# Gate logits of a two-level mixture of experts: products split over tokens and turned on VectorE, in place of products split over depth, a copy and a joining product

## The chip, the core and the metric

One core of one Trainium2 chip runs the whole kernel. The metric is device time in microseconds (us). Before the change the median of 3 runs is 469.96 us (469.8 to 470.32). The engines are TensorE (PE; its weight loads are shown apart as PEld), VectorE (DVE), ScalarE (ACT), GpSimd (POOL) and SyncE (SP). They run side by side, each through its own queue in order, and wait for one another by semaphores.

## What is computed

Multi-query attention over 8 batches of 384 tokens with 16 heads of 64, followed by a mixture of experts on the 3072 resulting tokens of width 1024, with 4 groups of 4 experts:

```python
scores = scale * q @ k.T                       # one k and v for all heads
attn = softmax(scores)
x = (attn @ v) as (3072, 1024)
g_logits = x @ w_group                         # 4 columns
g_idx, g_w = argmax and its softmax weight
e_logits = x @ w_expert[g_idx]                 # 4 columns for each of 4 groups
e_idx, e_w = argmax and its softmax weight
out[token] = g_w * e_w * relu(x @ w1[g_idx, e_idx]) @ w2[g_idx, e_idx]
```

For each token, therefore, 4 group logits and 4 x 4 expert logits are wanted: 20 numbers out of a depth of 1024. These 20 logits are what the change is about.

## The kernel before

**Tiling and stages.** A step `p` is one block of 128 tokens of one batch with all 16 heads (24 steps of 128 tokens): `b, st = divmod(p, 3)`. Within a step TensorE makes the scores in six pieces of 64 keys (`scores`, L251), ScalarE exponentiates each (L253), VectorE adds them up (L259, L261, L265), and TensorE multiplies the pieces of the step before by v (`values`, L290). `weigh` (L301) divides by the row sums and leaves x, transposed, in `xT`: partitions are 128 of the 1024 depth positions, then 8 such slices `ko`, then the 384 tokens of a batch. GpSimd makes a bf16 copy of it (L302).

**Expert work as filler.** From step 4 on each step ends with four or five *units* of the expert products of an earlier batch (`fill`): a first layer unit is 8 products of 128x384 and a relu on ScalarE (L416, L417), a second layer unit 8 products of 128x512 and a scaled copy on ScalarE (L424, L425). Each batch is run through one expert chosen by its first block of tokens; leftover tokens of other experts are gathered at the end.

**The gate before.** At the end of the second step of a batch (`st == 1`) three jobs are put between the last units, at the places n-3, n-2 and n-1 of n units (L611 to L617):

- `gate_a` multiplies xT by `gw`, the gate weights (8 slices of 128 x 32 columns, of which 20 are used and 12 are zero). The array is taken as four column groups of 32. The depth is what is split: group j takes slice j, then slice j + 4, over all tokens of the batch (L314). So the PSUM tile `gps` has, on partitions 32j to 32j+31, a part of the sum for every token. ScalarE copies it to `part` (L316).
- `gate_both` adds the four parts up and turns the result in one: for each block of 128 tokens a product with `part` as the weights and `sel` (four identities of 32 under one another) as the moving operand (L321). In `lps` the tokens are on the partitions. Then `choose_a` copies the first block's 20 logits to `L` (L368) and finds each token's expert (L330 to L334), and for the batch before, whose blocks 1 and 2 are now complete, `gate_logits` copies the other 40 and `gate_math` finds the expert and its weight (L373 to L391, with an exponential on ScalarE, L380).
- `counts` adds the choices up over the tokens by a product with ones (L342), ScalarE copies the counts (L346), and `choose_b` finds the commonest expert and starts to load its weights (L356 on).

The tile `xT` is one for all batches. A gate with `lo = 0, hi = 3` at batch b therefore reads block 0 of batch b and, in the same tile, blocks 1 and 2 of batch b-1, which is why one gate serves two batches. There are nine gates: for the first block alone (in step 2, as jobs between score and value products), seven full ones, and one for the last two blocks at the end (L625 to L628).

**PSUM.** `scores`, `gps`, `lps`, the counts and the units take their PSUM tiles in turn from one ring of three (`ps_s`): the fourth tile waits until the first has been read. The order is written out by hand (`manual_schedule`): each engine's queue holds its instructions in the order in which the program calls them.

**The head.** `load_first` loads k on ScalarE's queue (L123), and four pieces of the first q block on SyncE's (L127), followed by the other blocks (L129 on). TensorE runs warming products on ones meanwhile (L152, L451).

Of the kernel before, what the change touches and what calls it, by code (L numbers as in the profile page):

```python
# [9 lines left out]
FP32 = mybir.dt.float32  # L10
# [3 lines left out]
P = 128  # L14
ACTF = mybir.ActivationFunctionType
OP = mybir.AluOpType
AX = mybir.AxisListType.X
# [4 lines left out]
def kernel(  # L22
# [11 lines left out]
    nc = tc.nc  # L34
    B, H, S, D = q.shape
# [6 lines left out]
    ST = S // P  # L42
    KO = Dm // P
# [4 lines left out]
    CW = 512  # L48
# [27 lines left out]
    def side(shape, dtype, name):  # L76
        return ps_s.tile(shape, dtype, tag="s", name=name)
# [41 lines left out]
    def load_first():  # L119
        kt = pool.tile([P, ST, 2, D], FP32, tag="k", bufs=2, name="kn")  # L120
        qt = pool.tile([P, ST, HP, 2, D], FP32, tag="qraw", bufs=2, name="qn")
        for a in range(2):
            nc.scalar.dma_start(out=kt[:, :, a], in_=kn)  # L123
        for c in range(2):
            hs = slice(c * HC, (c + 1) * HC)
            for a in range(2):
                nc.sync.dma_start(out=qt[:, 0, hs, a], in_=qn[0, :, a, hs])  # L127
        for a in range(2):
            nc.sync.dma_start(out=qt[:, 1, :, a], in_=qn[1, :, a])  # L129
        k_raw[0], q_raw[0] = kt, qt  # L130
        load_k(1)
        load_v(0)
        for a in range(2):
            nc.sync.dma_start(out=qt[:, 2, :, a], in_=qn[2, :, a])
        qe_in = q[1].rearrange("(a hp) (st p) d -> st p a hp d", a=2, p=P)
        qe = pool.tile([P, HP, 2, D], FP32, tag="y", bufs=4, name="qe")
        for a in range(2):
            nc.sync.dma_start(out=qe[:, :, a], in_=qe_in[0, :, a])
        q_nat.append(qe)
# [150 lines left out]
                nc.tensor.matmul(out=o_ps[p][64 * a:64 * a + 64, c, :], lhsT=v_sb[b][r, j, :], rhs=pt[p, j][r, a, :], start=(j == 0), stop=(j == KB - 1))  # L290

    xT_all = pool.tile([P, KO, S], FP32, tag="xT", bufs=1, name="xT")
    part_all = pool.tile([P, S], FP32, tag="part", bufs=1, name="part")

    def weigh(p):
        b, st = divmod(p, ST)
# [6 lines left out]
        if st == ST - 1:  # L303
            nc.sync.dma_start(out=xb_dram[b], in_=xbf[b][:].rearrange("p k s -> p (k s)"))

    part, ohe_t, choice, logits, seen = {}, {}, {}, {}, {}

    def gate_a(b, lo, hi):
        n = (hi - lo) * P
        ps = side([P, CW], FP32, "gps")  # L310
        for r in range(2):
            for j in range(4):
                ko = 4 * r + j
                nc.tensor.matmul(out=ps[32 * j:32 * j + 32, 0:n], lhsT=gw[:, ko, :], rhs=xT[b][:, ko, lo * P:hi * P], start=(r == 0), stop=(r == 1), tile_position=(0, 32 * j))  # L314
        part[b] = part_all
        nc.scalar.copy(out=part[b][:, lo * P:hi * P], in_=ps[:, 0:n])  # L316

    def gate_b(b, lo=0, hi=ST):
        ps = side([P, ST, 32], FP32, "lps")
        for st in range(lo, hi):  # L320
            nc.tensor.matmul(out=ps[:, st, :], lhsT=part[b][:, st * P:(st + 1) * P], rhs=sel[:], start=True, stop=True)  # L321
        return ps

    first = {}

    def choose_a(b, ps):
        gate_logits(b, ps, 0, 1)
        L = logits[b][:, 0]
        mx = pool.tile([P, 5], FP32, tag="mx1", bufs=1, name="mx1")
        nc.vector.reduce_max(out=mx[:], in_=L, axis=AX)  # L330
        oh = pool.tile([P, 5, 4], FP32, tag="oh1", bufs=1, name="oh1")
        nc.vector.tensor_tensor(out=oh[:], in0=L, in1=mx[:].unsqueeze(2).to_broadcast([P, 5, 4]), op=OP.is_ge)
        ohe = pool.tile([P, 4, 4], BF16, tag="ohe1", bufs=1, name="ohe1")
        nc.vector.tensor_mul(out=ohe[:], in0=oh[:, 1:5, :], in1=oh[:, 0, :].unsqueeze(2).to_broadcast([P, 4, 4]))  # L334
        first[b] = ohe
# [26 lines left out]
        wts[b] = (w1, w2)  # L362
        choice[b] = idx

    def gate_logits(b, ps, lo, hi):
        if lo == 0:
            logits[b] = pool.tile([P, ST, 5, 4], FP32, tag="L", bufs=2, name="L")
        nc.vector.tensor_copy(out=logits[b][:, lo:hi].rearrange("p s a e -> p s (a e)"), in_=ps[:, lo:hi, 0:20])  # L368

    def gate_math(b):  # L370
        L = logits[b]
        mx = pool.tile([P, ST, 5], FP32, tag="mx", bufs=1, name="mx")
        nc.vector.reduce_max(out=mx[:], in_=L[:], axis=AX)  # L373
        mxb = mx[:].unsqueeze(3).to_broadcast([P, ST, 5, 4])
        oh = pool.tile([P, ST, 5, 4], FP32, tag="oh", bufs=1, name="oh")
        nc.vector.tensor_tensor(out=oh[:], in0=L[:], in1=mxb, op=OP.is_ge)
        dl = pool.tile([P, ST, 5, 4], FP32, tag="dl", bufs=1, name="dl")
        nc.vector.tensor_sub(out=dl[:], in0=L[:], in1=mxb)
        ex = pool.tile([P, ST, 5, 4], FP32, tag="ex", bufs=1, name="ex")
        nc.scalar.activation(out=ex[:], in_=dl[:], func=ACTF.Exp)  # L380
        ohe = pool.tile([P, ST, 4, 4], BF16, tag="ohe", bufs=1, name="ohe")
        nc.vector.tensor_mul(out=ohe[:], in0=oh[:, :, 1:5, :], in1=oh[:, :, 0, :].unsqueeze(3).to_broadcast([P, ST, 4, 4]))
        ohe_t[b] = ohe
        smx = pool.tile([P, ST, 5], FP32, tag="smx", bufs=1, name="smx")
        nc.vector.reduce_sum(out=smx[:], in_=ex[:], axis=AX)
        ri = pool.tile([P, ST, 5], FP32, tag="ri", bufs=1, name="ri")
        nc.vector.reciprocal(out=ri[:], in_=smx[:])
        tt = pool.tile([P, ST, 4], FP32, tag="tt", bufs=1, name="tt")
        nc.vector.tensor_mul(out=tt[:], in0=ri[:, :, 1:5], in1=ri[:, :, 0:1].to_broadcast([P, ST, 4]))
        gv = gate_all[:, b * GE:(b + 1) * GE, :].rearrange("p (g e) s -> p s g e", g=G)  # L390
        nc.vector.tensor_mul(out=gv, in0=ohe[:], in1=tt[:].unsqueeze(3).to_broadcast([P, ST, 4, 4]))  # L391
# [68 lines left out]
    def fill(n):  # L460
        while n > 0:
            if not units:
                if begun[0] >= B or begun[0] not in wts:
                    return
                units.extend(first_units(begun[0]))
                begun[0] += 1
            units.pop(0)()
            n -= 1
            ran[0] += 1
            if ran[0] == (FO + 2 * ST) * (B - 2) + FO:  # L470
                leftover_w1()
            if ran[0] == (FO + 2 * ST) * (B - 1):
                leftover_w2()

    def gate_both(b):
        ps = gate_b(b)
        choose_a(b, ps)
        gate_logits(b - 1, ps, 1, ST)
        gate_math(b - 1)

    def jobs_gates(b):
        if b == 0:
            return [lambda: gate_a(0, 0, 1), lambda: choose_a(0, gate_b(0, 0, 1)), lambda: counts(0, None)]
        return [lambda: gate_a(b, 0, ST), lambda: gate_both(b)]

    bound = {}
    oki = singles.tile([1, 1], I32, name="oki")
# [60 lines left out]
        leftover["w2"] = w2  # L548
    for p in range(NP):
        b, st = divmod(p, ST)  # L550
        jobs = jobs_gates(0) if p == 2 else []
        if p == 0 or p == ST or (st == 1 and 1 < b < B - 1):
            load_q(b + 1)
        for j in range(3):
# [47 lines left out]
        if p > ST:  # L602
            n = 5 if p in FIVES else 4
            steps = {}
            if p == NP - 1:
                bound_a()
            if st == 2:
                steps = {0 if b == 1 else 1: lambda: counts(None, b - 1)}
                if p == NP - 1:
                    steps = {0: lambda: (counts(None, b - 1), early_pair()), n - 1: bound_b}  # L610
            if st == 1:  # L611
                gate_a_, gate_b_ = jobs_gates(b)
                steps = {n - 3: gate_a_, n - 2: gate_b_, n - 1: lambda: counts(b, None)}
            for i in range(n):
                fill(1)
                if i in steps:
                    steps[i]()  # L617
# [4 lines left out]
    weigh(NP - 1)  # L622
    last = B - 1
    fill(2)
    gate_a(last, 1, ST)  # L625
    fill(1)
    gate_logits(last, gate_b(last, 1, ST), 1, ST)
    gate_math(last)  # L628
    fill(2)
    counts(None, last)  # L630
# [143 lines left out]
    with rare_block:  # L774
# [7 lines left out]
      with tc.If(ok < 1):  # L782
# [41 lines left out]
          nc.vector.memset(zero[:], 0.0)  # L824
          for b in range(B):
              xT_all = pool.tile([P, KO, S], FP32, tag="xT", bufs=1, name="xT")
              part_all = pool.tile([P, S], FP32, tag="part", bufs=1, name="part")
              xT[b] = xT_all
              for a in range(2):
                  nc.sync.dma_start(out=xT[b][a * D:(a + 1) * D], in_=xr[b, a])  # L830
              xg = pool.tile([P, KO, S], BF16, tag="xbf", bufs=2, name="xg")
              nc.vector.tensor_copy(out=xg[:], in_=xT[b][:])
              nc.sync.dma_start(out=xb_dram[b], in_=xg[:].rearrange("p k s -> p (k s)"))
              gate_a(b, 0, ST)
              gate_logits(b, gate_b(b), 0, ST)
              gate_math(b)
              for st in range(ST):
                  nc.sync.dma_start(out=outv[b, :, st, :], in_=zero[:])
# [33 lines left out]
```

## Time and profile before

| what | value |
|---|---|
| median time | 469.96 us |
| span of the profiled execution | 468.4 us |
| VectorE busy | 304.6 us, 483 instructions |
| ScalarE busy | 246.9 us, 360 instructions |
| gate products L314 | 144 records, 12.2 us, mean 456 ns |
| joining products L321 | 48 records, 6.2 us, mean 263 ns |
| ScalarE copies L316 | 9, 4.0 us, mean 445 ns |
| VectorE copies L368 | 16, 3.0 us, mean 186 ns |
| transposes on VectorE, 128x1024 (L243) and 128x384 (L233) | mean 1226 ns and 540 ns |
| granted TensorE clock | 0.996 |

How to read it: an fp32 product is two records of TensorE, since it runs in two passes; products on different column groups overlap, so that the sum of their records is more than the time that they take. The end of a product's record is modelled[...]; the distance from start to start is what a stream of products costs. In a row of cost groups the numbers after the bar are the busy time in us and the mean of one in ns, then the engine's idle time just ahead of these instructions and what ended most of it. In a timeline line, the start and the time are in us, "x16" counts the merged instructions, and the bracket gives the idle time of the engine before it and what released it.

### The profile page before, as it was taken

The page shows a single profiled execution, that of the slowest core. Times are in us where ns is not written, and L with a number is a line of the kernel's source. Part 1 is how long each engine was busy: PE and PEld are TensorE (multiplying, and loading weights), DVE is VectorE, ACT ScalarE, POOL GpSimd, SP SyncE. Part 2 cuts the span into 40 slices and gives each one's busy share as a digit, 9 for nine tenths or more (in the row PEclk, how much of TensorE's full clock was granted, in tenths as well). Part 3 has the DMA queues.
Part 4 walks back from the last instruction along what each step waited for, and adds up shares of the span by engine and source line. Part 5 has one row for each costly group of instructions (what it writes and reads, how often), then busy time and mean ns, then how long its engine had stood idle before and what let it go on. Part 6 is the DMA issues. An engine that isn't in the chain of part 4 may idle for free. (4 is left out here: it accounts for less than half of the span.)

```text
span 468.4 us, 9356 instructions
## 1 busy us (share of the span) xinstructions
PE 457.0 (98%) x3791; PEld 195.5 (42%) x3807; DVE 304.6 (65%) x483; ACT 246.9 (53%) x360; POOL 60.4 (13%) x83
## 2 busy tenths in 40 slices
PE   8999999999999999999999999999999999999992
PEld 6333434433443344433434334434344334444641
DVE  4999958585695586783695855964858836682500
ACT  2966646546455555555474564664555654623331
POOL 1004003000130003000030000300021000330000
PEclk9999999999999999999999999999999999999997
DMA  8787997969499492967879493994929831499992
GB/s 161 94 135 117 218 211 118 212 165 215 77 161 232 168 167 33 201 132 237 134 102 211 123 210 88 147 211 171 156 60 197 151 158 46 63 208 261 283 247 79
DMA packets 152163, 74.52 MB, mean 159 GB/s; under 512 B 120216, under 2 KB 138652, under 8 KB 152112
## 3 DMA queue, kind: packets, MB, share of 16 engines
q0 software_dynamic: 28416, 37.84, 47.1%
q1 hardware_dynamic: 122896, 35.81, 32.4%
q8 instruction: 32, 0.52, 0.5%
q10 hardware_dynamic: 800, 0.20, 0.2%
q14 instruction: 19, 0.16, 0.1%
HBM read 92.62 MB, written 19.01 MB: 238 GB/s over the span
## 5 line engine op out<-in xcount | busy, mean ns | idle before, releaser
L253 ACT ACTIVATE pt<-s 128x1024 f32<-128x1024 f32 x144 | 142.8, 1025 | 62.7 <-PE s L251 60.1
L251 PE MATMUL s<-qT,kT 64*64 64x512 f32 x1152 | 144.6, 597 | 0.3 <-ACT qT L229 0.2
L290 PE MATMUL o<-pt,v 64*64 64x512 f32 x1152 | 141.0, 590 | 0.0
L261 DVE TENSOR_TENSOR presum<-presum,pt 128x1024 f32<-128x1024 f32 x96 | 116.6, 1215 | 14.0 <-ACT pt L253 8.2
L416 PE MATMUL hps<-xbf,w 128*128 128x384 bf16 x512 | 89.5, 326 | 0.6 <-ACT hT L417 0.6
L424 PE MATMUL yps<-w,hT 128*128 128x512 bf16 x368 | 84.9, 379 | 0.8
L290 PEld LDWEIGHTS o<-pt,v 64*64 64x64 f32 x1152 | 43.4, 133 | 76.6 <-issue 76.1
L259 DVE TENSOR_TENSOR presum<-pt 128x1024 f32<-128x1024 f32 x24 | 29.1, 1212 | 66.8 <-ACT pt L253 66.6
L425 ACT ACTIVATE y<-yps,gsel 128x512 f32<-128x512 f32 x48 | 33.0, 687 | 67.8 <-PE yps L424 64.2
L416 PEld LDWEIGHTS <-w 128*128 128x128 bf16 x512 | 48.0, 99 | 44.1 <-issue 14.8
L251 PEld LDWEIGHTS s<-qT,kT 64*64 64x64 f32 x1152 | 38.9, 133 | 65.5 <-issue 52.6
L302 POOL CAST xbf<-xT 128x1024 bf16<-128x1024 f32 x24 | 25.0, 1041 | 294.7 <-DVE xT L301 294.7
L417 ACT ACTIVATE hT<-hps 128x384 bf16<-128x384 f32 x64 | 31.2, 488 | 56.1 <-PE hps L416 48.3
L424 PEld LDWEIGHTS <-hT 128*128 128x128 bf16 x384 | 36.5, 98 | 50.3 <-issue 8.5
L145 POOL DMA_DIRECT2D w<-in_moe_w_dram x36 | 24.8, 708 | 70.9 <-issue 52.4
L301 DVE TENSOR_TENSOR xT<-o,rinv 128x1024 f32<-128x1024 f32 x24 | 29.2, 1216 | 2.6 <-PE o L290 2.6
L280 DVE STREAM_TRANSPOSE rinv<-rc 128x1024 f32<-128x1024 f32 x24 | 29.9, 1245 | 0.8
L265 DVE TRANSPOSE_TENSOR_REDUCE fold<-presum 128x32 f32<-128x1024 f32 x24 | 29.6, 1232 | 0.0
L368 DVE COPY L<-lps 128x20 f32<-128x20 f32 (+1 forms) x16 | 3.0, 186 | 34.5 <-PE lps L321 34.5
L243 DVE STREAM_TRANSPOSE qT<-qraw 128x1024 f32<-128x1024 f32 x20 | 24.5, 1226 | 0.6
L209 ACT ACTIVATE qraw<-qraw 128x1024 f32<-128x1024 f32 x21 | 22.0, 1049 | 0.0
L273 PEld LDWEIGHTS sm<-fold,sel 64*64 64x64 f32 x192 | 7.2, 133 | 12.9 <-issue 12.9
(146 smaller groups left out, 166.5 us busy)
## 6 DMA issues: line engine op xcount, KB each, us to landing
w<-in_moe_w_dram POOLq DMA_DIRECT2D x36, 512.0 KB, 10.0
w<-in_moe_w_dram POOLq DMA_DIRECT2D x9, 2048.0 KB, 22.1
out_dram<-y SPq DMA_DIRECT2D x24, 512.0 KB, 4.0
qraw<-in_q_dram SPq DMA_DIRECT2D x56, 192.0 KB, 3.8
x_bf<-xbf SPq DMA_DIRECT2D x8, 768.0 KB, 4.3
v<-in_v_dram SPq DMA_DIRECT2D x16, 96.0 KB, 2.9
k<-in_k_dram SPq DMA_DIRECT2D x28, 48.0 KB, 2.7
qn<-in_q_dram SPq DMA_DIRECT2D x4, 256.0 KB, 4.8
```

Of the source, the lines that this page charges most:

```text
L251: nc.tensor.matmul(out=ps[64 * c:64 * c + 64, a, :], lhsT=kT[b][r, j * D:(j + 1) * D], rhs=qT[p][r, c * CW:(c + 1) * CW], start=True, stop ...
L253: nc.scalar.activation(out=t[:], in_=ps[:], func=ACTF.Exp, scale=scale)
L259: nc.vector.tensor_add(out=presum[p][:], in0=pt[p, 0][:], in1=pt[p, 1][:])
L261: nc.vector.tensor_add(out=presum[p][:], in0=presum[p][:], in1=pt[p, j][:])
L265: nc.vector.tensor_reduce(out=fold[p][:], in_=presum[p][:].rearrange("p a (n i) -> p (a n) i", i=32), axis=AX, op=OP.add, apply_transpose= ...
L280: nc.vector.transpose(out=t[:].rearrange("p (b i) -> p b i", i=32), in_=rc[:].rearrange("p c b -> p (c b)").unsqueeze(2).to_broadcast([P, ...
L290: nc.tensor.matmul(out=o_ps[p][64 * a:64 * a + 64, c, :], lhsT=v_sb[b][r, j, :], rhs=pt[p, j][r, a, :], start=(j == 0), stop=(j == KB - 1))
L301: nc.vector.tensor_mul(out=xT[b][:, :, ts], in0=o_ps[p][:].rearrange("p c (h n) -> p (c h) n", n=P), in1=rinv[p][:].rearrange("p (h n) -> ...
L416: nc.tensor.matmul(out=ps[:, 0:S], lhsT=w1[:, ko, fc * P:(fc + 1) * P], rhs=xb[:, ko, :], start=(ko == 0), stop=(ko == KO - 1))
L417: nc.scalar.activation(out=state["h"][:, fc, :], in_=ps[:, 0:S], func=ACTF.Relu)
L424: nc.tensor.matmul(out=ps[:], lhsT=state["h"][:, fo, st * P:(st + 1) * P], rhs=w2[:, fo, nh * CW:(nh + 1) * CW], start=(fo == 0), stop=(fo ...
L425: nc.scalar.activation(out=y, in_=ps[:], func=ACTF.Copy, scale=gs_of()[:, st:st + 1])
```

## The change

The gate product no longer splits the depth over the column groups but the tokens: group j takes, of each block of 128 tokens, the 32 tokens 32j to 32j+31 (the `rhs` view with `j=4, i=32`), and goes through all 8 depth slices, so that each group ends with whole sums. `gps` is then, in each 32x32 block, logits by tokens, and a VectorE transpose that works on 32x32 blocks turns it straight out of PSUM into `L`, with the tokens on the partitions. The copy to `part`, the joining product and the PSUM tile `lps` go. `L` has 32 columns a block instead of 20, and its readers take a view of 20. The gate becomes one job in place of two, at the place n-2. In the fallback path at the end, which isn't entered with these inputs, the same functions are called. Apart from this, one of the four first loads of q is issued from ScalarE's queue instead of SyncE's.

It is meant to take the joining product off TensorE and the copy off ScalarE.

```diff
         for c in range(2):
             hs = slice(c * HC, (c + 1) * HC)
             for a in range(2):
-                nc.sync.dma_start(out=qt[:, 0, hs, a], in_=qn[0, :, a, hs])
+                (nc.scalar if c and a else nc.sync).dma_start(out=qt[:, 0, hs, a], in_=qn[0, :, a, hs])
...
     def gate_a(b, lo, hi):
-        n = (hi - lo) * P
-        ps = side([P, CW], FP32, "gps")
-        for r in range(2):
+        ps = side([P, ST * 32], FP32, "gps")
+        for ko in range(KO):
+            rhs = xT[b][:, ko, :].rearrange("p (s j i) -> p j s i", j=4, i=32)
             for j in range(4):
-                ko = 4 * r + j
-                nc.tensor.matmul(out=ps[32 * j:32 * j + 32, 0:n], lhsT=gw[:, ko, :], rhs=xT[b][:, ko, lo * P:hi * P], start=(r == 0), stop=(r == 1), tile_position=(0, 32 * j))
-        part[b] = part_all
-        nc.scalar.copy(out=part[b][:, lo * P:hi * P], in_=ps[:, 0:n])
-
-    def gate_b(b, lo=0, hi=ST):
-        ps = side([P, ST, 32], FP32, "lps")
-        for st in range(lo, hi):
-            nc.tensor.matmul(out=ps[:, st, :], lhsT=part[b][:, st * P:(st + 1) * P], rhs=sel[:], start=True, stop=True)
+                nc.tensor.matmul(out=ps[32 * j:32 * j + 32, lo * 32:hi * 32], lhsT=gw[:, ko, :], rhs=rhs[:, j, lo:hi, :], start=(ko == 0), stop=(ko == KO - 1), tile_position=(0, 32 * j))
         return ps
+
+    def gate_logits(b, ps, lo, hi):
+        if lo == 0:
+            logits[b] = pool.tile([P, ST, 32], FP32, tag="L", bufs=2, name="L")
+        nc.vector.transpose(out=logits[b][:, lo:hi, :].rearrange("p s e -> p (s e)"), in_=ps[:, lo * 32:hi * 32])
...
-    def gate_logits(b, ps, lo, hi):
-        if lo == 0:
-            logits[b] = pool.tile([P, ST, 5, 4], FP32, tag="L", bufs=2, name="L")
-        nc.vector.tensor_copy(out=logits[b][:, lo:hi].rearrange("p s a e -> p s (a e)"), in_=ps[:, lo:hi, 0:20])
-
     def gate_math(b):
-        L = logits[b]
+        L = logits[b][:, :, 0:20].rearrange("p s (a e) -> p s a e", a=5)
...
-    def gate_both(b):
-        ps = gate_b(b)
+    def gates(b):
+        if b == 0:
+            choose_a(0, gate_a(0, 0, 1))
+            return
+        ps = gate_a(b, 0, ST)
         choose_a(b, ps)
         gate_logits(b - 1, ps, 1, ST)
         gate_math(b - 1)
-
-    def jobs_gates(b):
-        if b == 0:
-            return [lambda: gate_a(0, 0, 1), lambda: choose_a(0, gate_b(0, 0, 1)), lambda: counts(0, None)]
-        return [lambda: gate_a(b, 0, ST), lambda: gate_both(b)]
...
-        jobs = jobs_gates(0) if p == 2 else []
+        jobs = [lambda: gates(0), lambda: None, lambda: counts(0, None)] if p == 2 else []
...
             if st == 1:
-                gate_a_, gate_b_ = jobs_gates(b)
-                steps = {n - 3: gate_a_, n - 2: gate_b_, n - 1: lambda: counts(b, None)}
+                steps = {n - 2: lambda: gates(b), n - 1: lambda: counts(b, None)}
...
     fill(2)
-    gate_a(last, 1, ST)
-    fill(1)
-    gate_logits(last, gate_b(last, 1, ST), 1, ST)
+    gate_logits(last, gate_a(last, 1, ST), 1, ST)
     gate_math(last)
```

## The prediction

> **What bounds the kernel now.** I read the busy shares first, then the waits of TensorE, then the timeline around one gate, because a change of 2 us in a stage of 55 us shows in no average. From the page, with two of its rows of cost groups:
>
> ```profile
> span 468.4 us, 9356 instructions
> ...
> PE 457.0 (98%) x3791; PEld 195.5 (42%) x3807; DVE 304.6 (65%) x483; ACT 246.9 (53%) x360; POOL 60.4 (13%) x83
> ...
> L368 DVE COPY L<-lps 128x20 f32<-128x20 f32 (+1 forms) x16 | 3.0, 186 | 34.5 <-PE lps L321 34.5
> ```
>
> TensorE is busy 98% of the span and no other engine above 65%. VectorE sat idle 34.5 us ahead of the gate's copies (some 4.3 us for each of eight gates): it waits for the gate, not the gate for it. The view of waits agrees; TensorE's products wait 3.5 us in all, nearly all of it at the head and the tail, and its weight loads show one wait that recurs at the gates:
>
> ```profile
> PE hps L416 <- ACT hT L417: 0.6, 1, 0.6
> ...
> PEld s L251 <- ACT cnt L346: 4.3, 5, 0.9
> ```
>
> So time is TensorE's queue, and a change is worth what it takes out of that queue plus what it does to this wait. The timeline of the second batch's gate (start, duration, engine, line, operation, tiles) shows both:
>
> ```profile
> 67.83 1.50 PE L314 MATMUL gps<-xT,gw 128*32 128x384 f32 x16
> ...
> 69.26 1.47 PE L416 MATMUL hps<-xbf,w 128*128 128x384 bf16 x8
> 69.39 0.48 ACT L316 COPY part<-gps 128x384 f32<-128x384 f32 x1 [0.97 <-PE gps L314]
> 70.41 0.80 PEld L321 LDWEIGHTS lps<-sel,part 128*128 128x128 f32 x6
> 70.57 0.75 PE L321 MATMUL lps<-sel,part 128*128 128x32 f32 x6
> ...
> 71.36 0.18 DVE L368 COPY L<-lps 128x20 f32<-128x20 f32 x1 [3.23 <-PE lps L321]
> ...
> 72.70 0.22 DVE L378 TENSOR_TENSOR dl<-L,mx 128x60 f32<-128x60 f32 x1
> ...
> 72.95 0.25 ACT L380 ACTIVATE ex<-dl 128x60 f32<-128x60 f32 x1 [1.69 <-DVE dl L378]
> 73.11 0.47 ACT L417 ACTIVATE hT<-hps 128x384 bf16<-128x384 f32 x1
> 73.48 0.16 ACT L346 COPY cnt<-cps 128x16 f32<-128x16 f32 x1
> 73.63 0.21 PEld L251 LDWEIGHTS s<-qT,kT 64*64 64x64 f32 x8 [0.87 <-ACT cnt L346]
> ```
>
> A gate takes TensorE twice (L314 and L321), with an expert unit between to hide the copy. And from the joining product (L321) a chain runs through VectorE to `ex`, behind which ScalarE's relu (L417) stands, behind which the PSUM buffer of the second score tile (L251, 73.63) comes free.
>
> Single records of this gate, the starts only: gate products start in four waves of four at 67.828, 68.175, 68.497 and 68.820; so 0.322 us a wave of 384 columns. The last expert product before started at 67.572 and the first after at 69.258; less one expert pitch (0.163) the gate product costs **1.523 us**: four waves (1.288) and 0.235 for entering and leaving the 128x32 tile mode. For the joining product the same two starts are 70.406 and 71.156: **0.587 us**. The other six full gates repeat these to 0.005 us.
>
> **What the Trainium skill says.** TensorE: Matmul & The Clock Gate, Part 3 (Packing small matmuls): products on different column groups run together, some 4 ns apart. Here they start 7 ns apart, four to a wave, so it holds. TensorEngine Tiling (Array Packing), Key Properties: a change of tiling mode drains TensorE. The trace agrees: a 0.09 us hole on each side of the gate product. The first page again, Back-to-back issue gap: a warm product costs its columns over 2.4 GHz plus 2.5 ns. In fp32 the trace fits twice the columns: 128 give 0.1095 us a wave (first gate), 256 give 0.216 (last), 384 give 0.322. VectorE: DVE Perf Modes, The three transpose paths: VectorE turns 32x32 blocks only, which is all that is asked here; no run so far shows one that reads PSUM.
>
> **The change, part by part.**
>
> *Joining product (3 products, 6 records), ScalarE copy.* Seven full gates give back 0.587 each. In the first gate the joining product stands between score and value products (31.336 to 32.193, less 0.429 for a score pitch): 0.428. In the last, between w2 products (428.327 to 428.906, less 0.213): 0.366. The copies (9 x 0.445 = 4.0 us of ScalarE) I cost at nothing: an expert unit of 1.3 us hid each.
>
> *Gate product, same multiplications in narrower pieces.* Before: 2 depth halves x 2 fp32 passes = 4 waves of 384 columns. After: 8 depth slices x 2 passes = 16 waves of 96 columns. By the fit a wave takes 2 x 96 / 2.4 + 2.6 = 82.6 ns, so 1.322 in place of 1.288, and with the same 0.235 of mode changes 1.557. Two things could make a wave longer. Its four weight loads: a load's record lasts 110 ns, which as a limit is the upper bound. I don't take it, since the denominators' product (L273, 64 columns of weights) starts successive waves 28 ns apart though its load records last 133 ns; most of a record is latency. And the moving operand now comes in three pieces of 32 columns, 128 apart, which no product of before does; I take no cost and keep a doubled wave (165 ns) as the bound. First gate: 16 waves at about 28 ns (the L273 pitch) for four at 109.5, 0.45 against 0.44; last: 16 at 56 for four at 216, 0.90 against 0.86. Both cost nothing within 0.05 us.
>
> *VectorE.* The copies of 20 and 40 columns (173 to 199 ns) become transposes of 32 and 64. A transpose of 1024 columns takes 1.226 us and of 384 0.540, so 1.07 ns a column and 0.13 fixed: 0.165 and 0.20; with what copies from PSUM take for the fixed part (0.15 to 0.157) 0.19 and 0.22. Upper bound: the 384-column transpose, 0.54 each. I take the middle pair, +0.04 us in the chain. The reads of `L` now skip 12 of 32 columns; same element counts, nothing. In the first gate the choice moves ahead of two additions on VectorE, which runs without a gap there (29.2 to 34.9) and only changes order.
>
> *The wait that stays.* The gate moves to where the joining product was (one unit before the counts), so the chain starts from it. Before, from the last joining product (71.044) to the second score tile (73.636) is 2.592. After: the last gate wave's record should last about 0.25 (against 0.276), so VectorE starts some 0.03 sooner and ends 0.04 later; 2.60. Behind the gate TensorE resumes after 0.178 (0.08 stream, 0.094 drain, as at 69.258 for 384 columns) instead of 0.112, and all that it does until the score tile is the same; so the interval from gate to second score tile stays, and 0.06 more of mode change hides in the wait. Queued behind a longer chain: `ex`, the relu, the count's copy on ScalarE, and TensorE's scores behind these.
>
> *Sum.* Full gate: 0.587 + 1.523 - 1.557 + 0.06 = 0.61; seven are 4.28. First 0.43, last 0.366 - 0.01 = 0.36. Together 5.07 us of a queue that is the bound: 469.96 - 5.07 = **464.9 us**.
>
> *The moved load at the head* (a fourth piece of q issued by ScalarE instead of SyncE). Issued about 0.5 us sooner, but TensorE's own warm-up runs to 5.98 and its q products follow at a steady 0.109, so nobody waits. ScalarE's table load comes 0.5 later, still 2.5 us before its first copy at 6.95. Nothing. *The tail* keeps its number of expert units; one moves behind the leftover's steps.
>
> **Rivals.**
>
> *Waves bound by their loads* (110 ns): 16 x 0.0274 = 0.44 us a full gate, 3.1 in seven: 468.0. For it: wave and load alternate in the trace at 109.5 with 128 columns. Against: that is also the stream's time, and the L273 waves.
>
> *Slower than before: the split stream.* If three short pieces halve the reading rate, a full gate gains 1.32 us, 9.3 in all: 474.2. Nothing in the trace shows such a read, for or against. Akin: dispatch. The same TensorE page (Wait — 56ns, not 53.3ns?) gives 62 ns a product for its sequencer with hardware decode off; 64 records, less 16 issued ahead (the trace's lead is never over 17), would be 48 x 0.062 = 2.98 against 1.32: 476.6. Against: in the last product (L719) the sequencer reached the branch behind all 32 products 0.147 us after the first started; with 16 or 17 queued, the rest went out at some 10 ns each.
>
> *The chain takes it all.* With transposes of 0.54 from PSUM the chain grows by 0.71, TensorE waits that much longer for its score tile at seven gates, and the gain drops by 5.0: 469.9, no change. Against: copies from PSUM here cost what copies from SBUF cost (173 ns for 20, 170 for 32).
>
> *More than the sum.* One PSUM buffer and one ScalarE entry fewer a gate could shorten other waits; if the remaining wait (some 0.17 a gate) went as well, 463.7.
>
> **How the numbers follow.** Forecast 0.70; load-bound 0.12; more 0.06; slower 0.08; no change 0.04. The range takes in the load-bound case and the larger gain, 463.6 to 468.4, and leaves out 0.12. Faster by over 0.2% (below 469.0): 0.88; within: 0.04; slower: 0.08.
>
> **What would show it.** Right: 16 waves about 83 ns apart, 1.3 to 1.35 us from first to last gate start; no L321; transposes of about 0.2 us; second score tile about 2.6 us after the last gate wave; stages shorter by 0.6 us each. Wrong: waves at 110 or 165 ns; transposes over 0.35 us; a wait of TensorE ahead of the counts, for `ohe`; or head and tail of another length.

## The result and the profile after

The changed kernel takes **466.36 us** (median of 4 runs, 466.23 to 466.55), beside 469.98 for the kernel before (4 runs): a ratio of 0.9923, 95% interval 0.9905 to 0.994. It is faster by 3.6 us where 5.1 were forecast. Run again later, on another occasion and beside other runs of before, it took 466.09 against 470.46: 0.9912 (0.9897 to 0.9927), so 4.4 us.

The page of the changed kernel, the same rows as before (L318 is the transpose that took the place of the copy L368):

```profile
span 464.9 us, 10115 instructions
...
PE 452.9 (97%) x4175; PEld 197.6 (43%) x4191; DVE 305.4 (66%) x483; ACT 243.0 (52%) x351; POOL 60.4 (13%) x83
...
L318 DVE STREAM_TRANSPOSE L<-gps 128x32 f32<-128x32 f32 (+1 forms) x16 | 3.6, 227 | 27.9 <-PE gps L312 27.9
```

TensorE has 384 more matmul records and is still busy 4.1 us less; the joining product's line is gone. VectorE's 16 turns cost 0.6 us more than the 16 copies did. The timeline of the gate that was shown for before:

```profile
69.02 1.53 PE L312 MATMUL gps<-xT,gw 128*32 128x96 f32 x64
...
70.48 1.47 PE L407 MATMUL hps<-xbf,w 128*128 128x384 bf16 x8
...
70.62 0.22 DVE L318 STREAM_TRANSPOSE L<-gps 128x32 f32<-128x32 f32 x1 [2.59 <-PE gps L312]
...
71.39 0.24 DVE L318 STREAM_TRANSPOSE L<-gps 128x64 f32<-128x64 f32 x1
...
72.05 0.22 DVE L369 TENSOR_TENSOR dl<-L,mx 128x60 f32<-128x60 f32 x1
...
72.30 0.25 ACT L371 ACTIVATE ex<-dl 128x60 f32<-128x60 f32 x1 [2.68 <-DVE dl L369]
72.46 0.47 ACT L408 ACTIVATE hT<-hps 128x384 bf16<-128x384 f32 x1
...
72.83 0.16 ACT L342 COPY cnt<-cps 128x16 f32<-128x16 f32 x1
...
72.98 0.14 PEld L251 LDWEIGHTS s<-qT,kT 64*64 64x64 f32 x3 [0.88 <-ACT cnt L342]
```

One visit of TensorE instead of two, and the chain dl, ex, relu, score tile as before, now starting from the gate product. The view of TensorE's waits has one new entry, at the end of the kernel:

```profile
PE pb L674 <- DMA xe<-x_bf: 0.5, 1, 0.5
```

Where the gain was made and lost is best seen in the two traces laid over one another, counted from the first score product of each, at the first score product of a step:

```
gain against before, us:
after the first gate                     0.379
after the full gates 1 to 7              0.937  1.482  2.028  2.577  3.127  3.669  4.220
(the step behind each, its wait passed)  0.924  1.470  2.020  2.570  3.114  3.664
at the gather near the end (px)          3.874
```

So a full gate brings 0.556 and its wait takes back some 0.01; from the last full gate to the end the gain shrinks by 0.345. Ahead of the first score product the changed execution was 0.272 late (7.859 against 7.587 us). The three larger differences from the forecast lie there: in the full gates, behind the last one, and at the head.

### The profile page after: what moved, and what is told of

It is laid out like the page before. It is cut to its first block, busy times and chain, and to the rows that moved or that the text cites. A ratio compares the mean times of both kernels' runs of the same rounds, so it can differ in the third digit from the quotient of the medians.

```text
span 464.9 us, 10115 instructions
## 1 busy us (share of the span) xinstructions
PE 452.9 (97%) x4175; PEld 197.6 (43%) x4191; DVE 305.4 (66%) x483; ACT 243.0 (52%) x351; POOL 60.4 (13%) x83
## 5 line engine op out<-in xcount | busy, mean ns | idle before, releaser
L407 PE MATMUL hps<-xbf,w 128*128 128x384 bf16 x512 | 88.3, 326 | 0.6 <-ACT hT L408 0.6
L416 ACT ACTIVATE y<-yps,gsel 128x512 f32<-128x512 f32 x48 | 33.0, 687 | 67.5 <-PE yps L415 63.4
L407 PEld LDWEIGHTS <-w 128*128 128x128 bf16 x512 | 47.9, 98 | 41.5 <-issue 10.4
L318 DVE STREAM_TRANSPOSE L<-gps 128x32 f32<-128x32 f32 (+1 forms) x16 | 3.6, 227 | 27.9 <-PE gps L312 27.9
```

The costliest lines, as they stand in the source:

```text
L407: nc.tensor.matmul(out=ps[:, 0:S], lhsT=w1[:, ko, fc * P:(fc + 1) * P], rhs=xb[:, ko, :], start=(ko == 0), stop=(ko == KO - 1))
L416: nc.scalar.activation(out=y, in_=ps[:], func=ACTF.Copy, scale=gs_of()[:, st:st + 1])
```

## The experiments

Times are compared with the runs of the kernel before that shared the chip; traces with the profile of the kernel after (or before), counted from the first score product.

### The head: the moved load, or the clock

On the changed kernel, and the reverse on the kernel before:

```diff
-                (nc.scalar if c and a else nc.sync).dma_start(out=qt[:, 0, hs, a], in_=qn[0, :, a, hs])
+                nc.sync.dma_start(out=qt[:, 0, hs, a], in_=qn[0, :, a, hs])
```

> The changed kernel with the fourth load of q back on SyncE's queue; all else as changed. In the profile after the change the first scores start 0.27 us later than before, with the granted clock rising 0.57 us later (6.035 against 5.464 us from the start of the trace). Theory A: that is the phase of the clock's ramp in that execution and not the moved load; then the time stays at 466.4 (within 0.2), and the head's start follows the ramp, not the edit. Theory B: the moved load costs the head 0.27; then 466.1 and the first scores at 7.59 us.

> The kernel before with only the fourth load of q moved to ScalarE's queue. Theory A (clock phase): 470.0 within 0.2. Theory B (the moved load costs): 470.25.

Measured: 466.32 us with the load moved back (466.36 with it moved), and 470.07 beside 470.08 for the kernel before with it moved (ratio 1.0, 0.9992 to 1.0009). The moved load is worth nothing that the times can tell. The start of the first scores follows the moment at which the trace shows the granted clock rise from a half to full:

```
kernel                    clock rises   first score   (us from the trace's start)
before                    5.464         7.587
before, load moved        5.355         7.535
after                     6.035         7.859
after, load moved back    6.730         8.186
after, run again          5.750         7.725
```

> The changed kernel unchanged, beside the mended ones on the same chip, for the spread of its head: 466.4 within 0.3. Theory A: the first scores start at 7.587 us plus 0.475 times the distance of the clock's rise from 5.464 us, as in the other runs. Rival (the head follows the kernel): 7.86 as in its first profile, whatever the rise.

The last row had been forecast from the others: 7.587 + 0.475 x 0.286 = 7.723. In eleven of the thirteen profiles of this case the first score lies within 0.003 us of this line: each us of later rise costs it 0.475, whatever the kernel. The other two (rise at 4.138 and at 4.800) lie 0.34 and 0.46 us behind it, for a reason that comes below. The Trainium skill (TensorE: Matmul & The Clock Gate, Part 1, What's actually happening) says that the window which releases the clock runs free, so that the moment depends on where in it the first product falls; over all thirteen profiles here it lay between 4.14 and 6.73 us, though the first product always started at 1.34. The stretch at full clock then lasted a whole number of times 3.413 us in each (132 to 135), which fits a window of fixed length. When the rise came at 4.138, in the run with one unit moved (below), TensorE waited for the loads of q instead:

```profile
PE qps L228 <- DMA qn<-in_q_dram: 0.5, 1, 0.5
```

There the moved load does show. On ScalarE's queue it is issued 0.48 us sooner (2.13 us in place of 2.62), but it lands later, at 6.44 to 6.78 us in ten profiles against 6.28 to 6.50 in the three that have it on SyncE's queue, and the piece ahead of it at 6.02 to 7.04 against 5.68 to 5.79. Four of the profiles with the moved load, with a rise at 4.14 to 5.36, start the fifth product of q 0.13 to 0.68 us behind its turn, just after the later of these two pieces; the one with a rise at 4.44 and the load unmoved does so by 0.16.

So the head's 0.27 is chance of one execution. The execution with the load moved back shows the other end of it: its clock fell at 457.289 us, inside the very last products, and these took 1.86 us instead of 1.06. Over the thirteen profiles the first score lies between 7.10 and 8.19 us, and from the start of the last product to the end of the kernel it is 6.67 to 7.77 us, whatever the kernel. Single times of one kernel are spread by up to 2.3 us (before: 469.19 to 471.51); head and end can make up much of that, though only one or two executions of each kernel were traced. So the traces between first score and last product are the finer measure: 3.875 us of gain by them, between the 3.6 and the 4.4 of the medians. The profile of the changed kernel run again is within 0.01 us of the first at every step.

### TensorE's share alone: the joining product put back

Products of the joining product's size, one for each token tile of the gate, on constants, read by nobody:

```diff
+        jn = side([P, ST, 32], FP32, "jps")
+        for st in range(lo, hi):
+            nc.tensor.matmul(out=jn[:, st, :], lhsT=ident[:], rhs=sel[:], start=True, stop=True)
         ps = side([P, ST * 32], FP32, "gps")
```

> The changed kernel with products of the size of the joining products (128 columns of weights, 32 moving columns, fp32) put back on TensorE just ahead of each gate product, on constants, their result unread: TensorE's share of the old gate without its copy and without its place in the chain. Theory A (TensorE's queue is the bound, every product in it is paid): 0.587 at each of seven gates, 0.43 and 0.37 at the first and last, 4.9 in all: 471.2, and each stage longer by 0.58 to 0.59. Rival (part of it fills TensorE's waits): under 470.

Measured: 471.97 us. In the trace the first gate costs 0.414 more, each full gate 0.585 to 0.589, the last 0.373. Theory A holds to a few nanoseconds at the full gates: the queue is the bound and all of a product in it is paid. The time is 0.8 above the forecast, for other reasons: the wait for the leftover's load near the end is 1.1 us longer in this run, the head waits 0.3 for loads of q behind the first score, and a wait of 0.7 us behind the counts of one step (a product of L416 before, L407 after), which the kernels before and after have alike, is missing.

### ScalarE's share alone: a copy put back

Behind the gate product, of its PSUM tile:

```diff
+        part = pool.tile([P, ST * 32], FP32, tag="part", bufs=1, name="part")
+        nc.scalar.copy(out=part[:, lo * 32:hi * 32], in_=ps[:, lo * 32:hi * 32])
         return ps
```

> The changed kernel with ScalarE copying the gate product's PSUM tile to SBUF beside VectorE's transposes, its result unread: ScalarE's share of the old gate. Theory A (the copy lies beside other work): 466.4 within 0.3. Rival (ScalarE's queue is near its limit at the gate, where relu and exponential follow): 0.1 to 0.3 at each of seven gates, 467.1 to 468.5.

Measured: 468.39 us, outside the forecast, and some 0.27 a gate. But the run doesn't measure what it was meant to: VectorE's transpose waited for the copy of the same PSUM tile, which put the copy into the chain (0.15 of it is paid at the first score tile behind the gate, 0.12 at the second).

```profile
70.34 0.24 ACT L314 COPY part<-gps 128x96 f32<-128x96 f32 x1 [1.00 <-PE gps L312]
70.61 0.22 DVE L320 STREAM_TRANSPOSE L<-gps 128x32 f32<-128x32 f32 x1 [2.86 <-ACT part L314]
```

So the copy was put back in another way, where the old one stood (one unit earlier) and with nobody waiting for it:

```diff
+    def idle_copy(b):
+        part = pool.tile([P, S], FP32, tag="part", bufs=1, name="part")
+        nc.scalar.copy(out=part[:], in_=xT[b][:, 0, :])
...
-                steps = {n - 2: lambda: gates(b), n - 1: lambda: counts(b, None)}
+                steps = {n - 3: lambda: idle_copy(b), n - 2: lambda: gates(b), n - 1: lambda: counts(b, None)}
```

> The changed kernel with a ScalarE copy of 128x384 fp32 (of x in SBUF, its result unread) at the place in the queue where the copy of the partial sums stood, one expert unit ahead of the gate, at the seven full gates; unlike the run with the copy behind the gate product, VectorE waits for nothing of it. Theory A (that copy lay beside other work): 466.4 within 0.3, and the distance from score to score as in the changed kernel within 0.02 us a stage. Rival (ScalarE's share was paid too): 0.3 to 0.5 at each of seven gates, 468.5 to 469.9.

Measured: 466.29 us, beside 466.09 for the changed kernel on the same chip, and no step of the trace moves by more than 0.01 against the profile after. The copy had cost nothing where it stood.

### The chain behind the gate: twice as many transposes, and none in the way

```diff
-        nc.vector.transpose(out=logits[b][:, lo:hi, :].rearrange("p s e -> p (s e)"), in_=ps[:, lo * 32:hi * 32])
+        for _ in range(2):
+            nc.vector.transpose(out=logits[b][:, lo:hi, :].rearrange("p s e -> p (s e)"), in_=ps[:, lo * 32:hi * 32])
```

> The changed kernel with each VectorE transpose of the gate done twice over. Theory A (the chain from the gate product through VectorE, the exponential and the relu sets when the second score tile may start, and is already the longer way): the two extra transposes, 0.22 and 0.24 with some 0.03 between, come through in full, 0.5 at each of seven gates, 3.5 in all: 469.9. Rival (VectorE is idle there and its work is hidden): 466.4.

Measured: 469.71 us. A full gate is 0.53 to 0.54 longer in the trace up to the second score tile: the second pair comes through in full (0.217, 0.250 and two gaps of 0.034), though VectorE is idle most of that time. Seven of these are 3.7 us; that the time meets the forecast of 3.5 more is in part luck, since this run also lacks 0.6 of the wait behind the counts of one step. The view of TensorE's waits shows, seven times 0.34:

```profile
PE s L251 <- DVE L L319: 2.4, 7, 0.3
```

This is the wait of the first score tile, not of the second that theory A speaks of. That tile is the fourth in the ring of three behind `gps` and takes its PSUM buffer, which the last transpose reads until 72.22 us; the tile starts at 72.37. So 0.41 of the 0.53 shows at the first tile already, and 0.12 at the second. In the changed kernel as it is the last transpose ends at 71.63 and the first tile starts at 71.89, so by the same lag of 0.15 it has 0.12 to spare (an estimate).

Then the opposite: the exponential, and what needs it, behind the counts, so that the relu of the last unit no longer stands behind it.

```diff
     def gate_math(b):
...
-        ex = pool.tile([P, ST, 5, 4], FP32, tag="ex", bufs=1, name="ex")
-        nc.scalar.activation(out=ex[:], in_=dl[:], func=ACTF.Exp)
         ohe = pool.tile([P, ST, 4, 4], BF16, tag="ohe", bufs=1, name="ohe")
...
         ohe_t[b] = ohe
+        diff[b] = dl
+
+    def gate_weights(b):
+        ohe, dl = ohe_t[b], diff[b]
+        ex = pool.tile([P, ST, 5, 4], FP32, tag="ex", bufs=1, name="ex")
+        nc.scalar.activation(out=ex[:], in_=dl[:], func=ACTF.Exp)
...
-                steps = {n - 2: lambda: gates(b), n - 1: lambda: counts(b, None)}
+                steps = {n - 2: lambda: gates(b), n - 1: lambda: (counts(b, None), gate_weights(b - 1))}
```

> The changed kernel with the exponential of the gate and what follows from it put behind the counts instead of ahead of the last expert unit's relu; nothing is left out. Theory A: the second score tile waits some 0.17 us, plus 0.05 of a broken stream, at each of seven gates for the chain transpose, choice, exponential, relu; without it each gate gives 0.2 us, 1.4 to 1.6 in all: 464.9. Rival (the wait as the profile names it, for the counts' copy): that copy still ends some 1.0 us after the counts' product, so the score tile comes no sooner and the time stays 466.4.

Measured: **464.28 us** (0.9875 of before, 0.986 to 0.989). In the trace each full gate gives 0.22 to 0.23, 1.55 in all. The time fell by 2.1, more than forecast; as far as the profiled execution shows, the rest lies ahead of the first score and behind the last product, where executions of one kernel differ anyway. The timeline of the same gate, to be held against the one above:

```profile
71.68 0.49 ACT L414 ACTIVATE hT<-hps 128x384 bf16<-128x384 f32 x1 [2.37 <-PE cps L338]
...
72.07 0.17 ACT L342 COPY cnt<-cps 128x16 f32<-128x16 f32 x1
72.12 0.27 ACT L380 ACTIVATE ex<-dl 128x60 f32<-128x60 f32 x1
72.22 0.42 PEld L251 LDWEIGHTS s<-qT,kT 64*64 64x64 f32 x8 [0.43 <-ACT cnt L342]
```

The relu runs as soon as its products end, and the score tile follows the scores before it: its first product starts at 72.49, 0.91 behind that of the first tile (71.58), instead of 72.98 - 71.89 = 1.09; the line at 72.22 is its weight load alone. With the 0.05 that the wait costs in the wave behind it, this is the 0.23. The rival, that the score waits for the counts' copy by which the view names the wait, falls by the times: in all three timelines the weight load starts 0.05 us after the end of the relu (before 73.63 and 73.58, after 72.98 and 72.93, here 72.22 and 72.17) and 0.01 before the end of the counts' copy.

The same edit on the kernel before:

> The kernel before with the gate's exponential and what follows from it put behind the counts, as in the run on the changed kernel; nothing is left out. There the stage gave 0.225 a gate. Before the change the chain was 0.09 shorter beside the same work of TensorE less 0.066, so its wait for the second score tile was as long within 0.02: theory A gives 0.22 at each of seven gates here too, 1.5 in all: 468.5, and the change is then worth 0.58 to 0.6 a gate without the wait in play. Rival (the wait came with the change): 470.0.

Measured: 468.56 us (0.997 of before, 0.9957 to 0.9983), 0.22 a gate in the trace. The wait was there all along. And laid over one another, these two kernels without the wait differ by 0.384 at the first gate and by 0.557, 0.557, 0.556, 0.557, 0.556, 0.558 and 0.556 at the full ones: the change as it is in TensorE's queue, with nothing else in play.

### The end: one unit put back behind the leftover's load

One more expert unit between the leftover's load (it was issued further up) and the transposes of `xe` (L674) that need it:

```diff
-    fill(2)
+    fill(3)
```

> The changed kernel with one more expert unit ahead of the first transposes of the leftover's x near the end (fill(3) for fill(2)), so the number of units is the same. Theory A: the unit that the change moved behind the leftover's steps left TensorE waiting for the load of xe, 0.66 us in the profile (436.33 against 435.67 us); with a unit put back ahead of it the wait goes and the time is 465.7. Rival: the end is set by the leftover's own chain (loads, gather) and not by TensorE's queue; then 466.4 as it is.

Measured: 465.78 us (0.9906 of before, 0.989 to 0.9922), and 0.67 less from the last gate to the gather; the wait for `xe` is gone from the view of waits. In the profile after the load was issued at 428.68, landed 7.6 us later, and TensorE came to need it at 435.67; before, it was issued at 432.19, landed after 8.1 and was needed at 441.08, so 0.8 of slack.

Between the load and the transposes stand six units in both kernels. What the change shortened is the stretch ahead of the load, which reads what the store of the last x (`x_bf`) has written (SPq is SyncE's queue, which issues both). Before:

```profile
424.79 0.34 SPq L304 DMA_DIRECT2D x_bf<-xbf  x1
...
426.81 1.90 PE L424 MATMUL yps<-w,hT 128*128 128x512 bf16 x8
...
432.19 0.36 SPq L633 DMA_DIRECT2D xe<-x_bf  x1
```

After:

```profile
420.85 0.34 SPq L303 DMA_DIRECT2D x_bf<-xbf  x1
...
428.68 0.36 SPq L619 DMA_DIRECT2D xe<-x_bf  x1
...
436.33 0.62 PE L674 MATMUL pb<-ident_bf,xe 128*128 128x128 bf16 x8 [0.50 <-DMA xe<-x_bf]
```

After the change the load goes out 0.02 us behind the landing of the store (428.66), as in all its variants but the one with the joining product put back; before, the store had landed (432.00) by the time SyncE reached the load. Store and load one behind the other take 15.4 us after and 15.5 before, counted from the issue of the store to the landing of the load. TensorE came to need the load 14.8 us behind the issue of the store after, and 16.3 before. The unit at 426.81, between the two parts of the last gate, stood in this stretch and was taken out of it. The size of the wait is that of one execution: store and load landed after 6.8 to 8.7 and 6.8 to 9.5 us, and the view of waits gives 0.3 to 1.6 for the changed kernel and its variants without the unit.

### Both mends together

> The changed kernel with both mends together: the gate's exponential behind the counts, and one more expert unit ahead of the leftover's transposes. Theory A (the two waits are independent, 1.55 and 0.67 us in the traces): 466.4 - 1.55 - 0.67 = 464.1. Rival (the earlier arrival at the end finds the leftover's loads late, and the second gain is eaten by a new wait): 464.8, as with the exponential alone.

Measured: **463.91 us**, 0.9864 of before (0.9847 to 0.988), beside 466.09 for the changed kernel on the same chip. In the trace the gates give their 1.58 and the end its 0.67; 0.21 went at the start of this execution, whose clock rose early (4.711) and whose fifth product of q then had to wait for a load (landed at 6.48, product at 6.57). The two waits are independent.

## Why the prediction held, and what it missed

**The bound**: right. The joining product comes back at 0.587 a gate when it is put back, to within 0.002, and 0.414 and 0.373 at the ends (0.428 and 0.366 had been read off). A full gate product costs 0.030 more than before (1.716 against 1.686 us from the product ahead of it to the one behind), and 0.587 less 0.030 is the 0.557 that the two kernels without the wait differ by.

**The narrow waves**: right. From first to last start the full gate's products take 1.282 us, less 0.045 for the start and for the four groups: 15 steps of 82.5 ns, where the fit gave 82.6; the last gate's take 55.8 (56). Neither the weight loads nor the moving operand in three pieces limits them, so the two rivals that rested on these, and dispatch with them, fall: 64 records started within 1.282 us, 20 ns each. (The lead of at most 17 that the prediction used for dispatch doesn't fit its own reading of L719: when the branch behind the 32 products was reached, 8 of them had started.) Only the first gate's 32-column waves came in at 34.5 on average instead of 28, and its product costs 0.119 more than before (1.212 against 1.093) where 0.01 was forecast. The first gate gave 0.379, not less, since its joining product had cost more than was read off: 0.448, for the product ahead of it starts at 31.316 (31.336 is the last record of that wave), and 0.05 in a slower first wave behind it.

**ScalarE's copies and the moved load**: nothing in the times, as forecast. That the load, issued sooner, lands later was not foreseen.

**The step that failed most: the tail.** "Keeps its number of expert units; one moves behind the leftover's steps", and with that no cost. The unit had been part of what hid the store of x and the load of `xe` behind it. Where the last gate was to give 0.36, the end lost 0.345: a wait of 0.66 against a gain of 0.336 (0.366 less 0.030 for the gate product), and some 0.02 of small shifts; with the unit put back the same stretch gives 0.33. A move of filler was costed by what it adds up to, not by what it stood between. The prediction had named a tail of another length as a sign of being wrong, and that sign came.

**The step that was mis-sized: "the wait that stays".** The chain was to start 0.03 sooner and grow by 0.04. VectorE started 0.314 us after the last gate product's start, as it had after the last joining product, and the transposes took 0.217 and 0.243 instead of 0.19 and 0.22. From the last gate product to the second score tile it is 2.681 us, where 2.592 were before and 2.60 forecast. So the 0.06 of later resumption did not hide in the wait: 0.55 a gate instead of 0.61, 0.44 in seven.

The terms add up, as they must, each being what the traces show against the forecast: 0.44 in the full gates, 0.05 in the first, 0.70 at the end are 1.19, and 5.07 less 1.19 is 3.88; the traces show 3.875. That the range took these misses in is partly luck: it had been made wide for waves bound by their loads, which did not happen.

**Left open**: the wait of some 0.7 us ahead of one product behind the counts of one step. Eleven of the thirteen profiles have it, before and after alike, and in each of them the product starts 0.05 us after the end of the relu ahead of it (after: 246.06 and 246.01), by which the view names the wait. In the runs with the joining product put back and with twice the transposes the same product waits for VectorE's semaphore in place of ScalarE's and starts before that relu ends. Why the program is ordered otherwise there stays open. It plays no part in the difference.

## What to carry to other kernels

Where one engine's queue is the bound, a small operation is worth its start-to-start time in that queue, and at the full gates the trace before the change gave that to the hundredth of a us; spend the doubt on the waits. When an edit removes a stage and with it a slot of filler, look at each transfer that was issued ahead of that slot and is needed behind it, and at chains of them: here a store and the load that reads what it wrote. And when a short chain through other engines ends in a queue in order, ask what stands behind its last link: here an exponential that nobody needed yet held up the relu that everybody waited for, and moving it was worth more than a third of the change itself.

## What the runs showed of the hardware that was not expected

- A moving fp32 operand in three pieces of 32 columns (128 apart) streams as fast as contiguous ones let expect: 82.5 ns for a wave of 96 columns on four column groups, where the fit through contiguous 128, 256 and 384 columns gives 82.6.
- Waves of 32 fp32 columns on four column groups, sixteen in a row, came every 34.5 ns on average (31 to 48 apart in the profile after); two waves of 16 columns had come 28 apart.
- VectorE transposes out of PSUM: 128x32 in 0.217 us and 128x64 in 0.243. A line through these two (an estimate) is 0.8 ns a column over a fixed part of 0.19, larger than the 0.13 that the transposes out of SBUF gave. The first 128x32 of the kernel took 0.173; why is not shown.
- The moment of the clock's rise (4.14 to 6.73 us) moved the first score by 0.475 us for each us, unless a load was then the limit, and its fall caught the last products once (1.86 instead of 1.06 us).
- A load moved to another queue and issued 0.48 us sooner landed later, at 6.44 to 6.78 us against 6.28 to 6.50.
